# Routed attention and a Hyena gate on one core: q turned by VectorE, its loads and those of k, v, masks and reciprocals cut anew

## The chip, the cores and the metric

One core of a Trainium2 chip. Its engines: TensorE (PE, with its weight loads as PEld), VectorE (DVE), ScalarE (ACT), GpSimd (POOL) and SyncE (SP); sixteen DMA engines move data between HBM and the on-chip memory (SBUF). Matrix products end in PSUM banks, from which DVE and ACT take them. The metric is the device time of one execution in microseconds (us), as the median of several runs; lower is better.

## The reference

The kernel computes attention in which a query sees only keys of its own cluster, and passes the result through a Hyena gate:

```python
q_assign = np.argmax(np.einsum('bhsd,hcd->bhsc', q_n, c_n), axis=-1)   # nearest of 16 centroids
k_assign = np.argmax(np.einsum('bhsd,hcd->bhsc', k_n, c_n), axis=-1)
mask = q_assign[:, :, :, None] == k_assign[:, :, None, :]
scores = np.where(mask, scale * np.matmul(q, k.transpose(0, 1, 3, 2)), -1000000000.0)
scores = scores - np.max(scores, axis=-1, keepdims=True)
attn = np.exp(scores)
attn = attn / (np.sum(attn, axis=-1, keepdims=True) + 1e-09)
attn_out = np.matmul(attn, v)                        # [4, 8, 768, 64] -> x [4, 768, 512]
proj = x @ w_proj                                    # x1, x2, x3, 512 columns each
x2_conv = irfft(rfft(x2, axis=1) * rfft(filter_fft, axis=0), axis=1)
out = (x1 * x2_conv * x3) @ w_out                    # [4, 768, 512] float32
```

Batch 4, heads 8, sequence 768, head width 64, model width 512. Inputs and output are float32.

## The kernel before

**Tiling.** The 32 heads are worked in eight groups `n` of four, each of two pairs `pr` of heads; two groups make a batch `b`. A pair has six tiles `sk` of 128 keys. For a tile, PE makes the scores of 768 queries and two heads (bf16, in three banks `u`), ACT takes exp of them into `p` (float32), PE multiplies with `vraw` into the bank pair `pair`, and DVE adds `p` up in `acc` for the denominators. The first sum of a pair, of tiles 0 and 1 (line 699), can be DVE's or POOL's. After batch `b` follows its Hyena part (function `hyena`): projections, a Fourier transform as matrix products, its inverse, the output product; it runs beside the attention of later groups, the last one alone at the end.

**Loading and turning.** `load_qk` loads q (`j` = 0) and k (`j` = 1) of a pair into one of four buffers `qkraw`, `load_v` loads v into one of three buffers `vraw`; all by SP's queue, apart from a few early ones. A group needs four buffers, so a buffer is free for the next group when the present one has been turned. Scores need the width of the head on the partitions:

- q is turned by PE: six transposes of 128x128 per pair against `ident` (line 589), each three of them put into `qkP`/`qkT` by ACT or DVE (line 591, in helper `copy`, lines 245 and 247). The second half of the queries is turned with `ident` reversed, so it stands backwards.
- k of groups 2 to 7 (`TURN`) is turned by DVE in blocks of 32x32 (line 567). For that, k is loaded in runs of 32 numbers: four transfers per pair, each 32 partitions (line 286).
- v of groups 2 to 7 has its rows in an order that fits k's: four transfers of 32 partitions per pair (line 299).

Then `qkT` is cast to bf16 into `augs` (line 595; ACT, DVE or POOL), the operand of the scores.

**Routing.** Similarities to the centroids (line 609), turned and compared on DVE (lines 614 to 624), give a one-hot code `ohB`; with a product against `tri` it becomes two bf16 arrays in `ohT` (lines 635, 637). Eight transfers per group, 16 partitions each (line 474), put them as extra rows into `augs`, where they act as the mask. Of groups 0 and 1 some steps differ.

**Denominators.** For groups 0, 1 and 7 PE sums `acc` (line 716); for the others POOL's queue folds `acc` with adding transfers (line 736). By way of HBM (`dd`, `dp` or `dn`, line 728 to 742) the sums come to `dn`, 12 numbers in each of 128 partitions; DVE takes the reciprocal, it goes to `dr` in HBM (line 750), and two transfers (line 753) spread it as `rb` over 64 partitions for each head. Line 782 multiplies (`osb` + eps) by `rb` into `xT`, the operand of the Hyena part. `hyena` reads the backward half with a reversed view.

**Order.** There is no run-time scheduling. `build` lists all operations with their dependences; the list `ORDER` gives their sequence, each entry five times the operation's number plus the engine (PE, ACT, DVE, POOL, SP). Every engine works through its own part in that order and waits where a dependence is open, DMA issues on SP included: what stands behind a waiting issue waits as well. An operation of POOL marked `lock` waits for the last one of DVE that is marked so.

The k load and the reciprocals' spread, as they stand before:

```python
T.qkraw[s][64 * x + 32 * y:64 * x + 32 * y + 32]...rearrange("p (c d) -> p c d", d=32),
T.k[...+ x].rearrange("(p c) d -> p c d", c=4 * NT)[:, :, 32 * y:32 * y + 32]
...
T.rb[64 * hp:64 * hp + 64], T.dr[os][hp:hp + 1].to_broadcast([64, S])
```

Of the kernel before, what the change touches and what calls it, by code (L numbers as in the profile page):

```python
# [34 lines left out]
TURN = [(n, pr) for n in range(2, NG) for pr in range(2)]  # L35
FIRST = 2
# [191 lines left out]
def build(T):  # L228
# [22 lines left out]
    def ap(h):  # L251
        return bank(h.ids[0])
# [13 lines left out]
    def dma(e):  # L266
        return (T.nc.scalar if e == "ACT" else T.nc.sync).dma_start
# [995 lines left out]
```

## Time and profile before

| | |
|---|---|
| median of 3 runs | 369.12 us (366.23 to 370.4) |
| profiled execution, device time | 363.86 us |
| its span, first to last instruction | 362.1 us |
| mean granted TensorE clock | 0.997 |
| moved by DMA | 46.19 MB in 109,796 packets, 97,640 of them under 512 bytes |

The profile is of one execution. Its groups of instructions give the line, the engine, the operation, what is written from what, shape and count, then the busy time in us and the mean of one in ns, then the idle time of the engine just before them and what ended it. A matmul's end is modelled, so a busy PE is not PE at its peak. The transfers' rows give the issuing queue, the count, KB of each and the median time from issue to landing in us. A queue's share is the time that its packets took, as a share of sixteen engines' time.

### The profile page before, as it was taken

What the parts mean: (1) busy time and instruction counts of PE and PEld (TensorE: products, weight loads), DVE (VectorE), ACT (ScalarE), POOL (GpSimd) and SP (SyncE); (2) the same over time, 40 slices, a digit from 0 to 9 for tenths busy, and PEclk for the clock granted to TensorE, in tenths of its full rate; (3) what the DMA queues carried; (4) which work ended last, traced back from release to release, by engine and by line L of the source; (5) the groups of instructions that cost most, each with busy time, mean ns of one, the idle gap of its engine ahead of it and who ended that gap; (6) DMA issues with size and microseconds to landing.
All of it is one profiled execution on the core that took longest, in us unless ns stands there. A gap on an engine that the chain in (4) does not pass through costs nothing.

```text
span 362.1 us, 8441 instructions
## 1 busy us (share of the span) xinstructions
PE 349.1 (96%) x3197; PEld 200.6 (55%) x3200; DVE 335.0 (93%) x444; ACT 271.4 (75%) x516; POOL 113.0 (31%) x147
## 2 busy tenths in 40 slices
PE   8999996999999999999999999999999999999994
PEld 4555543444655555665455555576556765576672
DVE  6999996998999999999989999998999999999994
ACT  5998876896997987888998865767885677434452
POOL 5350062020003416220420266443112433025830
PEclk9999999999999999999999999999999999999998
DMA  7939796584668778678867779845446731310124
GB/s 175 221 94 168 156 200 140 113 164 114 137 132 152 117 147 135 126 155 143 151 99 171 134 112 176 201 86 118 86 64 175 144 45 46 103 45 3 61 115 176
DMA packets 109796, 46.19 MB, mean 128 GB/s; under 512 B 97640, under 2 KB 103484, under 8 KB 109756
## 3 DMA queue, kind: packets, MB, share of 16 engines
q1 hardware_dynamic: 104844, 35.59, 43.5%
q0 software_dynamic: 2752, 8.98, 17.3%
q10 hardware_dynamic: 2160, 1.08, 1.0%
q8 instruction: 25, 0.41, 0.5%
q14 instruction: 15, 0.12, 0.1%
HBM read 31.59 MB, written 7.40 MB: 108 GB/s over the span
## 4 chain that ended last, share of the span: by engine, by line
PE 75%; DVE 8%; ACT 7%; DMA 6%; issue 2%; SPq 1%; DVEq 0%; ACTq 0%
PE bank L157 31%; PE pair L690 28%; PE bank L817 6%; PE bank L155 2%; PE bank L589 2%; DMA dd<-den 2%; ACT p L679 2%; PE bank L609 2%; ACT p L676 2%; DMA aug<-ohT 1%; ACT aug L245 1%; DMA qkraw<-in_k_dram 1%; ACT ohT L635 1%; DMA qkraw<-in_q_dram 1%; DVE qkP L567 1%
## 5 line engine op out<-in xcount | busy, mean ns | idle before, releaser
L690 PE MATMUL pair<-p,vraw 128*64 128x385 f32 x768 | 142.1, 488 | 0.3 <-ACT osb L706 0.3
L679 ACT ACTIVATE p<-bank 128x512 f32<-128x512 f32 x192 | 110.1, 610 | 24.4 <-PE bank L157 21.3
L703 DVE TENSOR_TENSOR acc<-p,acc 128x1536 f32<-128x1536 f32 x64 | 112.2, 1753 | 2.9 <-ACT p L679 0.2
L157 PE MATMUL bank<-aug,aug 80*64 80x512 bf16 (+3 forms) x724 | 81.6, 326 | 4.8 <-ACT den L722 2.9
L690 PEld LDWEIGHTS pair<-p,vraw 128*64 128x64 f32 x768 | 55.8, 136 | 44.2 <-issue 35.9
L157 PEld LDWEIGHTS <-aug 80*64 80x64 bf16 (+1 forms) x724 | 44.5, 109 | 44.7 <-issue 31.2
L676 ACT ACTIVATE p<-bank 128x512 f32<-128x512 f32 x96 | 57.6, 610 | 7.2 <-PE bank L157 5.8
L736 POOL DMA_DIRECT2D acc<-acc x30 | 23.9, 815 | 97.5 <-DVE acc L703 64.1
L157 PE MATMUL bank<-xT,wpj 128*64 128x384 bf16 x472 | 44.9, 326 | 0.0
L157 PEld LDWEIGHTS <-wpj 128*64 128x64 bf16 x472 | 28.6, 110 | 13.1 <-issue 3.1
L247 POOL CAST aug<-qkP 64x768 bf16<-64x768 f32 x19 | 15.6, 820 | 52.2 <-DVE acc L703 22.3
L245 ACT CAST aug<-qkP 64x768 bf16<-64x768 f32 x37 | 30.6, 828 | 0.6
L847 DVE TENSOR_TENSOR tm<-bank,hm 128x512 f32<-128x512 f32 x44 | 28.3, 682 | 2.3 <-PE bank L452 1.0
L157 PEld LDWEIGHTS <-y 128*64 128x64 bf16 x456 | 23.1, 110 | 12.1 <-issue 2.9
L245 ACT COPY qkP<-bank 128x384 f32<-128x384 f32 x41 | 18.5, 485 | 8.7 <-PE bank L157 5.4
L157 PE MATMUL bank<-wout,y 128*64 128x512 bf16 (+1 forms) x200 | 23.9, 371 | 0.5 <-DVE y L939 0.5
L817 PE MATMUL bank<-wpj,xT 128*64 128x512 bf16 x192 | 22.4, 379 | 0.0
L939 POOL TENSOR_TENSOR y<-yy,x 128x768 bf16<-128x768 f32 x7 | 12.7, 1821 | 30.9 <-DVE yy L934 27.8
L699 POOL TENSOR_TENSOR acc<-p,p 128x1536 f32<-128x1536 f32 x5 | 17.3, 3465 | 6.7 <-ACT osb L706 4.0
L851 POOL TENSOR_TENSOR y<-tm 128x512 bf16<-128x512 f32 x13 | 16.4, 1272 | 9.2 <-DVE acc L703 3.9
L589 PE MATMUL bank<-ident,qkraw 128*128 128x128 f32 x120 | 18.4, 280 | 0.9 <-DMA qkraw<-in_q_dram 0.7
L699 DVE TENSOR_TENSOR acc<-p,p 128x1536 f32<-128x1536 f32 x11 | 19.1, 1740 | 0.0
(180 smaller groups left out, 437.9 us busy)
## 6 DMA issues: line engine op xcount, KB each, us to landing
qkraw<-in_q_dram SPq DMA_DIRECT2D x30, 192.0 KB, 3.8
rb<-dr SPq DMA_DIRECT2D x30, 192.0 KB, 3.1
qkraw<-in_k_dram SPq DMA_DIRECT2D x51, 96.0 KB, 3.3
vraw<-in_v_dram SPq DMA_DIRECT2D x48, 96.0 KB, 4.2
out_dram<-ob SPq DMA_DIRECT2D x9, 512.0 KB, 2.6
acc<-acc POOLq DMA_DIRECT2D x10, 384.0 KB, 4.6
acc<-acc POOLq DMA_DIRECT2D x10, 192.0 KB, 4.3
vraw<-in_v_dram SPq DMA_DIRECT2D x4, 384.0 KB, 4.6
```

The costliest lines, as they stand in the source:

```text
L157: T.nc.tensor.matmul(out[64 * i:64 * i + 64], lhsT[:, 64 * i:64 * i + 64], rhs, start=start, stop=stop)
L245: T.nc.scalar.copy(out, in_)
L589: T.nc.tensor.transpose(ap(h)[:, ts(t, 128)], raw(s, 3 * ch + t), T.ident[:, ::-1] if ch > j else T.ident)
L676: T.nc.scalar.activation(o, ap(h).rearrange("p (a b) -> p a b", a=2), Act.Exp, scale=0.125)
L679: T.nc.scalar.activation(flat(s)[:, lo:lo + 512], ap(h), Act.Exp, scale=0.125)
L690: T.nc.tensor.matmul(o[64 * hp:64 * hp + 64, ch, :385], T.vraw[vs][:, hp, sk * D:(sk + 1) * D], T.p[slots[sk]][:, hp, 384 * ch:384 * ch + ...
L699: alu(e).tensor_tensor(T.acc[os], T.p[slots[0]][:, :, :S], T.p[slots[1]][:, :, :S], op=Alu.add)
L703: T.nc.vector.tensor_tensor(T.acc[os], T.p[slots[sk]][:, :, :S], T.acc[os], op=Alu.add)
L736: op(("POOL", .8), lambda e, rows=rows: T.nc.gpsimd.dma_start(flat_()[:rows], flat_()[rows:2 * rows], accum_op=Alu.add), te, r=[], w=AK, b ...
L817: T.nc.tensor.matmul(ap(h)[64 * i:64 * i + 64], T.xT[xs][:, kt, c:c + 64], T.wpj[:, kt, DM:2 * DM], start=kt == 0, stop=kt == ND - 1)
L847: op(("DVE", .68), lambda e, i=i, cs=cs, r=r, h=h: T.nc.vector.tensor_tensor(T.tm[r][:, cs], ap(h), hmrow(i, (0, 2, 2, 3)[2 * r + cs]), op ...
L851: op({"POOL": 1.5, "DVE": .68}, lambda e, i=i, r=r: alu(e).tensor_tensor(T.y[:, i, r], T.tm[r][:, 0], T.tm[r][:, 1], op=Alu.add if r else ...
```

## The change

For groups 2 to 7, q is now turned by DVE as k is: 12 more turns on DVE, and no transposes and no evacuations for them. q of these groups is loaded with 8 transfers per pair in runs of 32 numbers, and stands forwards in both halves; so line 782 becomes two operations of half the width, the second of which writes backwards, and `xT` is as before. k takes two transfers per pair, v two, the masks four per group, the reciprocals one per pair. In the new loads of q, k and v and in the spread, the source is divided otherwise than the target: for k, a source of 2 x 768 x 32 goes to 64 partitions x 24 x 32.

`ohT` has no memory of its own any more: it lies in that of `sim`, with its two arrays side by side on 64 partitions, so a hit can write it when `sim` has been read, and `sim` waits for the masks' transfers. `den` has two buffers. Some early operations get the lock, the warm-up of PE names the memory that it uses, and a load of `wout` names one more dependence. `LATE` gives the same pairs as before, and `EXTRA` is empty. `ORDER` is new throughout, with 1,932 operations for 1,987; in it 8 first sums are POOL's (5 before), 11 products of line 939 (7 before), and 14 casts (19 before); ACT casts 48 times (37 before), DVE twice (8 before).

```diff
-        turned = j == 1 and (n, pr) in TURN
+        turned = (n, pr) in (TURNQ, TURN)[j]
+        parts = 1 if j else 4
         for x in range(2) if turned else ():
-            for y in range(2):
-                op(("SP", .6), lambda e, x=x, y=y: dma(e)(
-                    T.qkraw[s][64 * x + 32 * y:64 * x + 32 * y + 32].rearrange("p t h d -> p (t h d)").rearrange("p (c d) -> p c d", d=32),
-                    T.k[n // 2, 4 * (n % 2) + 2 * pr + x].rearrange("(p c) d -> p c d", c=4 * NT)[:, :, 32 * y:32 * y + 32]), due,
-                   w=[("qkraw", s, x, y)], byts=130e3, kind="load", after=after, lat=.8)
+            for g in range(parts):
+                def load(e, x=x, g=g):
+                    m = S // parts
+                    rows = (T.q, T.k)[j][n // 2, 4 * (n % 2) + 2 * pr + x, g * m:g * m + m].rearrange("t (y d) -> y t d", y=2)
+                    raw = T.qkraw[s][64 * x:64 * x + 64].rearrange("p t h d -> p (t h d)")[:, 768 // parts * g:768 // parts * (g + 1)]
+                    dma(e)(raw.rearrange("p (c d) -> p c d", d=32), rows)
...
     def load_v(n, pr, due, after=()):
-        for x in range(4) if (n, pr) in TURN else ():
+        for x in range(2) if (n, pr) in TURN else ():
             op(("SP", .6), lambda e, x=x: T.nc.sync.dma_start(
-                T.vraw[(2 * n + pr) % NV][32 * x:32 * x + 32], T.v[n // 2, 4 * (n % 2) + 2 * pr:4 * (n % 2) + 2 * pr + 2].rearrange(
-                    "h (i p t) d -> p i h (t d)", p=4, t=NT)[x]), due, w=[("vraw", (2 * n + pr) % NV, x)], byts=LOAD / 4, kind="load",
-               after=after, lat=.8)
+                T.vraw[(2 * n + pr) % NV][:, x], T.v[n // 2, 4 * (n % 2) + 2 * pr + x].rearrange("(i p t) d -> p i (t d)", p=4, t=NT)),
+               due, w=[("vraw", (2 * n + pr) % NV, x)], byts=LOAD / 2, kind="load", after=after, lat=.8)
...
+                to = slice(64 - 64 * hp, 80 - 64 * hp)
+                if n:
+                    rows = slice(32 * pr + 16 * hp, 32 * pr + 16 * hp + 16)
+                    out.append(op(("SP", .6), lambda e, a=a, hp=hp, rows=rows, to=to: dma(e)(T.aug[a][hp][to], T.ohT[rows]), due + .3 * hp,
+                                  r=OHT + SIM + [("zero", a, j) for j in range(2)], w=[("augm", a, hp, j) for j in range(2)], byts=50e3,
+                                  lat=2.0 if n < 3 else 1.0))
+                    continue
...
-            if (n, pr) in TURN and j:
+            if (n, pr) in (TURNQ, TURN)[j]:
                 if ch == 0:
-                    op(("DVE", .96), lambda e, s=s, z=z: V().transpose(
-                        T.qkP[z // 2][:, ts(1, S)], T.qkraw[s][:].rearrange("p t h d -> p (t h d)").rearrange("p (q t d) -> p t q d", q=4, d=32)),
-                       due, r=[("qkraw", s, h_, y) for h_ in range(2) for y in range(2)], w=qk(z, 0) + qk(z, 1))
+                    op(("DVE", .96), lambda e, s=s, z=z, j=j: V().transpose(
+                        T.qkP[z // 2][:, ts(j, S)], T.qkraw[s][:].rearrange("p t h d -> p (t h d)").rearrange("p (q t d) -> p t q d", q=4, d=32)),
+                       due, r=[("qkraw", s, x, y) for x in range(2) for y in range(4)], w=qk(z, 0) + qk(z, 1))
...
-            for hp in range(2):
-                op(("SP", .6), lambda e, hp=hp: T.nc.sync.dma_start(
-                    T.rb[64 * hp:64 * hp + 64], T.dr[os][hp:hp + 1].to_broadcast([64, S])), te + 9,
-                   r=[("dr", os)], w=[("rb", hp)], byts=196e3)
+            def spread(e):
+                x = T.dr[os][:]
+                T.nc.sync.dma_start(T.rb, bass.AP(tensor=x.tensor, offset=x.offset, ap=[list(x.ap[0]), [0, 64], list(x.ap[1])]))
+            op(("SP", .6), spread, te + 9, r=[("dr", os)], w=[("rb", 0), ("rb", 1)], byts=393e3)
...
+            def weigh(e, a_=a_):
+                for a in range(a_.start, a_.stop) if plain else [a_]:
+                    o, x, r = xv()[:, a], osv()[:, a], (ap(rk[a_.start])[:, :384] if plain else ap(rk[a_.start])[:, :384].unsqueeze(1)) if last else rbv()[:, a]
+                    if plain:
+                        o, x, r = (y.rearrange("p (t n) -> p t n", n=128) for y in (o, x, r))
+                        o = o[:, :, ::-1] if a else o
+                    T.nc.vector.scalar_tensor_tensor(o, x, eps(), r, op0=Alu.add, op1=Alu.mult)
...
+    T.aug = [[tl([128, 2, S], BF16, f"aug{i}{hp}") for hp in range(2)] for i in range(3)]
+    T.augs = [[[T.aug[i][hp][:, j] for j in range(2)] for hp in range(2)] for i in range(3)]
...
+    words = T.sim[:].rearrange("p a b -> p (a b)").bitcast(BF16)
+    T.ohT, T.ohT0 = words[:64].rearrange("p (j s) -> p j s", j=2), words[:, :S]
```

More of the change, by code (lines that the diff above doesn't have):

```diff
@@ L35 @@
 TURN = [(n, pr) for n in range(2, NG) for pr in range(2)]
+TURNQ = TURN
+LATE = [(n, pr) for n in (0, 1, NG - 1) for pr in range(2)]
+EXTRA = {}
 FIRST = 2
@@ L282, in load_qk @@
         src = lambda: (T.q, T.k)[j][n // 2, 4 * (n % 2) + 2 * pr:4 * (n % 2) + 2 * pr + 2].rearrange("h (p t) d -> p t h d", t=NT)
-        turned = j == 1 and (n, pr) in TURN
+        turned = (n, pr) in (TURNQ, TURN)[j]
+        parts = 1 if j else 4
         for x in range(2) if turned else ():
-            for y in range(2):
-                op(("SP", .6), lambda e, x=x, y=y: dma(e)(
-                    T.qkraw[s][64 * x + 32 * y:64 * x + 32 * y + 32].rearrange("p t h d -> p (t h d)").rearrange("p (c d) -> p c d", d=32),
-                    T.k[n // 2, 4 * (n % 2) + 2 * pr + x].rearrange("(p c) d -> p c d", c=4 * NT)[:, :, 32 * y:32 * y + 32]), due,
-                   w=[("qkraw", s, x, y)], byts=130e3, kind="load", after=after, lat=.8)
+            for g in range(parts):
[4 more added lines that the diff above has]
+                    dma(e)(raw.rearrange("p (c d) -> p c d", d=32), rows)
+                op(("SP", .6), load, due, w=[("qkraw", s, x, g)] if parts > 1 else [("qkraw", s, x, i) for i in range(4)],
+                   byts=260e3 / parts, kind="load", after=after, lat=.8)
         for x in range(2) if not turned else ():
@@ L306, in load_v @@
             T.vraw[(2 * n + pr) % NV], T.v[n // 2, 4 * (n % 2) + 2 * pr:4 * (n % 2) + 2 * pr + 2].rearrange(
-                "h (p t) d -> p h (t d)", t=NT)), due, w=[("vraw", (2 * n + pr) % NV, x) for x in range(4)], byts=LOAD, kind="load",
+                "h (p t) d -> p h (t d)", t=NT)), due, w=[("vraw", (2 * n + pr) % NV, x) for x in range(2)], byts=LOAD, kind="load",
            after=after, lat=.8 if n > 1 else 0.0)
@@ L464, in spectrum @@
                                        T.uv2[:, e, m], start=(m == 0), stop=(m == 2))
+    OHT = [("ohT", j, ch) for j in range(2) for ch in range(2)]
+    SIM = [("sim", ch, pr) for ch in range(2) for pr in range(2)]
     def masks(n, prs, due):
@@ L545, in first_masks @@
         op(("PE", .4), ohT, due + 1.0, r=[("oh", pr), "identb"], w=[h2], alloc=h2)
-        op(("DVE", .68), lambda e: V().tensor_scalar(r64(T.ohT), r64(ap(h2).bitcast(BF16))[:, :S], r64(T.mka), r64(T.mkb),
+        op(("DVE", .68), lambda e: V().tensor_scalar(r64(T.ohT0), r64(ap(h2).bitcast(BF16))[:, :S], r64(T.mka), r64(T.mkb),
                                                      op0=Alu.mult, op1=Alu.add), due + 1.1, r=[h2, "mk"],
-           w=[("ohT", pr)], free=[h2])
+           w=OHT + [("sim", ch, pr) for ch in range(2)], free=[h2])
         return masks(0, [pr], due + 1.2)
@@ L576, in tr2 @@
                         T.nc.tensor.transpose(bank(h.ids[i // 4])[:, ts(i % 4, 128)], raw(ss[i // NT], i % NT), T.ident[:, ::-1] if 3 <= i < NT else T.ident)
-                op(("PE", 1.42), tr2, due, r=[("qkraw", s, x, c) for s in ss for x in range(2) for c in range(2)] + ["ident"], w=[h], alloc=h)
+                op(("PE", 1.42), tr2, due, r=[("qkraw", s, x, c) for s in ss for x in range(2) for c in range(4)] + ["ident"], w=[h], alloc=h)
                 for c in range(3):
@@ L589, in tr @@
                         T.nc.tensor.transpose(ap(h)[:, ts(t, 128)], raw(s, 3 * ch + t), T.ident[:, ::-1] if ch > j else T.ident)
-                op(("PE", .58 if n == 0 else .36), tr, due, r=[("qkraw", s, x, c) for x in range(2) for c in ((0, 1) if n else (ch,))] + ["ident"] + ["cold"] * (n == 0), w=[h], alloc=h)
+                op(("PE", .58 if n == 0 else .36), tr, due, r=[("qkraw", s, x, c) for x in range(2) for c in (range(4) if n else (ch, ch + 2))] + ["ident"] + ["cold", ("wpj", 0)] * (n == 0), w=[h], alloc=h)
                 op(EV384 if n != 1 else {"ACT": .48}, lambda e, z=z, ch=ch, h=h: copy(e, T.qkT[z][:, ch], ap(h)[:, :384]),
@@ L594, in routing, with cast @@
                 for hp in range(2):
-                    op({"ACT": .82, "DVE": .65, "POOL": .95}, lambda e, a=ring(n, pr), hp=hp, j=j, z=z: copy(
-                        e, T.augs[a][hp][j][64 * hp:64 * hp + 64],
-                        T.qkT[z][64 * hp:64 * hp + 64].rearrange("p a b -> p (a b)")), due + 8 if n else due + 6,
+                    def cast(e, a=ring(n, pr), hp=hp, j=j, z=z):
+                        copy(e, T.augs[a][hp][j][64 * hp:64 * hp + 64], T.qkT[z][64 * hp:64 * hp + 64].rearrange("p a b -> p (a b)"))
+                    op({"ACT": .82, "DVE": .65, "POOL": .95}, cast, due + 8 if n else due + 6,
                        r=qk(z, 0) + qk(z, 1) + [("zero", ring(n, pr), j)],
@@ L637, in hits @@
                         V().tensor_scalar(o, x, -1.0 if j else -BIG, 0.0 if j else -BIG, op0=Alu.mult, op1=Alu.max if j else Alu.add)
-                op({"ACT": .47, "DVE": .55}, hits, due - 1.6 + .1 * ch, r=[h], w=[("ohT", j, ch)], free=[h])
+                op({"ACT": .47, "DVE": .55}, hits, due - 1.6 + .1 * ch, r=[h], w=[("ohT", j, ch), ("sim", ch, j)], free=[h])
         masks(n, range(2), due + 1.3)
@@ L651, in attention @@
         last = (n, pr) == (NG - 1, 1)
+        extra = EXTRA.get((n, pr), 0)
         os, o3 = kt % 2, (2 * n + pr) % 3
@@ L693, in pv @@
                                            start=(sk == 0), stop=(sk == NT - 1))
-            op(("PE", 1.3), pv, due, r=[("p", slots[sk], u) for u in range(3)] + [("vraw", vs, x) for x in range(4)] + ["eps"] +
+            op(("PE", 1.3), pv, due, r=[("p", slots[sk], u) for u in range(3)] + [("vraw", vs, x) for x in range(2)] + ["eps"] +
                ([ob] if sk else []), w=[ob], alloc=None if sk else ob, kind="pv")
@@ L855, in hyena @@
             op(("ACT", .83), lambda e: T.nc.scalar.activation(T.neg, T.inv[:].rearrange("p (c b) x -> p c b x", c=2)[:, :, 2:], Act.Copy, scale=-1.0), A(80),
-               r=INV, w=["neg"] + [("qkraw", 0, x, c) for x in range(2) for c in range(2)])
+               r=INV, w=["neg"] + [("qkraw", 0, x, c) for x in range(2) for c in range(4)])
         gs, inv = [], []
@@ L1070, in weights @@
                 T.wout[:, i], T.w_out.rearrange("(t p) m -> p t m", p=128)[:, i]), 118 + 7 * i,
-                w=[("wout", i)] + [("fw", 2, 0), ("fw", 2, 1)] * (i == 0), byts=262e3, after=[first[0]], kind="load")
+                w=[("wout", i)] + [("fw", 2, 0), ("fw", 2, 1)] * (i < 2), byts=262e3, after=[first[0]], kind="load")
     WPJ = [("wpj", i) for i in range(ND)]
@@ L1202 @@
     T.dn, T.rb, T.dp = tl([128, 12], F32, "dn"), tl([128, S], F32, "rb"), tl([128, ROWS, 12], F32, "dp")
-    T.den = tl([128, 384], F32, "den")
+    T.den = [tl([128, 384], F32, f"den{i}") for i in range(2)]
     T.dd = [dram.tile([ROWS, 2 * S], F32, name=f"dd{i}") for i in range(2)]
```

56 lines of the change are left out of this document (28 added, 28 removed), and 162 rows, old and new, of the table ORDER.

## The prediction

> **What bounds the kernel now.** I read the engine totals first, then the chain of waits, then the stages, then the transfers.
>
> ```profile
> span 362.1 us, 8441 instructions
> PE 349.1 (96%) x3197; PEld 200.6 (55%) x3200; DVE 335.0 (93%) x444; ACT 271.4 (75%) x516; POOL 113.0 (31%) x147
> PE 75%; DVE 8%; ACT 7%; DMA 6%; issue 2%; SPq 1%; DVEq 0%; ACTq 0%
> 156.00:196.00 40.00, 39.70 (x377) 22.06 (x375) 37.73 (x45) 37.30 (x70) 7.89 (x9) 1.00 0.79 148
> 196.00:236.00 40.00, 39.95 (x352) 21.88 (x351) 38.47 (x53) 27.95 (x54) 18.15 (x16) 1.00 0.80 153
> q1 hardware_dynamic: 104844, 35.59, 43.5%
> q0 software_dynamic: 2752, 8.98, 17.3%
> ```
>
> The kernel is bound by PE, with DVE close behind (93%); transfers make 6% of the chain. The two stage rows (from:to us, length, busy PE, PEld, DVE, ACT, POOL, granted clock, DMA share, GB/s) say the same of the middle, and one thing more: there the sixteen DMA engines are already busy 79 to 80% of the time, mostly on SP's queue, q1. An edit that takes work from PE pays; one that makes transfers longer has little room. The loads of groups 2 to 7 lie here:
>
> ```profile
> L286 SPq DMA_DIRECT2D qkraw<-in_k_dram x48: 565/640/4904, 34.2 to 240.9; - x48
> qkraw<-in_q_dram SPq DMA_DIRECT2D x30, 192.0 KB, 3.8
> qkraw<-in_k_dram SPq DMA_DIRECT2D x51, 96.0 KB, 3.3
> ```
>
> The first k load of group 2 is issued at 34.2 us, the last of group 7 at 240.9 us. It lands 3.3 us later, so 362.1 - 244.2 = 118 us of work follow.
>
> **The compute that moves.** The rows that price it:
>
> ```profile
> L589 PE MATMUL bank<-ident,qkraw 128*128 128x128 f32 x120 | 18.4, 280 | 0.9 <-DMA qkraw<-in_q_dram 0.7
> L567 DVE STREAM_TRANSPOSE qkP<-qkraw 128x768 f32<-128x768 f32 x12 | 11.4, 960 | 0.0
> L245 ACT COPY qkP<-bank 128x384 f32<-128x384 f32 x41 | 18.5, 485 | 8.7 <-PE bank L157 5.4 <-PE bank L589 3.0
> L782 DVE SCALAR_TENSOR_TENSOR xT<-osb,rb 128x768 bf16<-128x768 f32 x15 | 15.2, 1012 | 0.6 <-DMA rb<-dr 0.6
> L782 DVE SCALAR_TENSOR_TENSOR xT<-osb,bank 128x384 bf16<-128x384 f32 x2 | 1.2, 612 | 0.1
> L245 ACT CAST aug<-qkP 64x768 bf16<-64x768 f32 x37 | 30.6, 828 | 0.6
> L247 DVE CAST aug<-qkP 64x768 bf16<-64x768 f32 x8 | 4.4, 550 | 0.1
> L699 DVE TENSOR_TENSOR acc<-p,p 128x1536 f32<-128x1536 f32 x11 | 19.1, 1740 | 0.0
> L699 POOL TENSOR_TENSOR acc<-p,p 128x1536 f32<-128x1536 f32 x5 | 17.3, 3465 | 6.7 <-ACT osb L706 4.0 <-ACT x L245 2.4 <-DVE y L851 0.2
> L939 DVE TENSOR_TENSOR y<-yy,x 128x768 bf16<-128x768 f32 x5 | 4.8, 953 | 0.2 <-POOL yy L934 0.2
> L939 POOL TENSOR_TENSOR y<-yy,x 128x768 bf16<-128x768 f32 x7 | 12.7, 1821 | 30.9 <-DVE yy L934 27.8
> ```
>
> PE loses the q transposes of six groups, 12 pairs of heads with 6 each: 72 of 120, that is 72/120 x 18.4 = 11.0 us, most of it on the path. ACT and DVE lose their 24 evacuations (24 x 0.485 = 11.6 us). DVE gets 12 more turns, 12 x 0.960 = 11.5 us, and 11 of the weighings of line 782 become two of half width: 11 x (2 x 0.612 - 1.012) = 2.3 us; that the second half is now written backwards is in no row, and I take nothing for it, with 11 x 0.6 = 7 us as the other end, were its time doubled. Read off the new order (a number is five times the operation's place plus its engine), DVE is relieved elsewhere: three first sums go to POOL (-3 x 1.740 = -5.2), four products of line 939 (-4 x 0.953 = -3.8), six casts (-6 x 0.550 = -3.3). That is +1.5 us for DVE, still under PE. POOL takes 3 x 3.465 + 4 x 1.821 = 17.7 us and has 113 of 362 filled; ACT takes casts of 0.828 us for what it loses. The double `den`, the locks on small early operations and the masks' new place in `sim` (a group lies between its writers) I cost at nothing, within 1 us: cover is POOL's idle time and the 36 us of a group. If the transfers cost nothing, this alone gives 363.9 - 11.0 = 353 us for the profiled execution.
>
> **The transfers.** This decides. A load of k was 32 target rows from 32 source rows; now it is 64 target rows, with a source whose outermost dimension is 2 (the halves y). A q load has the same 2, in quarters. The reciprocals' source has an outermost 2 before a repeat of 64; v's has 4. One transfer of the kernel before is of that kind: `dn<-dd` (line 730), 4 x 32 x 12 into 128 rows. Its opposite is `dr<-dn` (line 750), the same 128 packets of 48 bytes, with 128 rows on both sides. First `dr<-dn` in the window 64.27 to 64.50 us, then `dn<-dd` in 58.65 to 59.00 us; each digit is the mean busy share of sixteen engines, in tenths, over a fortieth of the window:
>
> ```profile
> DMA  0002464657778654555776355433430221101000
> DMA packets 144, 0.01 MB, mean 27 GB/s; under 512 B 144, under 2 KB 144, under 8 KB 144
> q1 hardware_dynamic: 144, 0.01, 39.9%
> ...
> DMA  0101121322911221010000000101212122222232
> DMA packets 90, 0.00 MB, mean 12 GB/s; under 512 B 90, under 2 KB 90, under 8 KB 90
> q1 hardware_dynamic: 90, 0.00, 18.2%
> ```
>
> The first is through in 0.23 us, 128 packets and 16 completions, up to 8 tenths of the engines at once. The second has moved fewer than 90 packets after 0.35 us and stands at 2 tenths, under 4/16, but for one slice: it runs on four engines. So the outermost source dimension of 4 confines it, however many target rows there are. By the same reading q, k and the reciprocals go to two engines, v to four. The Trainium skill, "DMA: Bandwidth & Descriptors", section "Why a DMA increments its semaphore by 16 and not by 1", says it as a rule: the number of engines is the largest one up to 16 that divides the slowest dimension of both sides. The trace agrees, 4 and 16. Were it the target alone that counts, the sum would stay at 353 us; that is a rival below.
>
> What a packet costs, from windows in which one kind ran (nearly) alone: a k load, 79.17 to 79.82 us; a reciprocal, 318.5 to 319.5; v, 131.85 to 132.60; and last 30 to 250 us for everything.
>
> ```profile
> DMA packets 823, 0.10 MB, mean 159 GB/s; under 512 B 823, under 2 KB 823, under 8 KB 823
> q1 hardware_dynamic: 823, 0.10, 101.6%
> ...
> q1 hardware_dynamic: 99, 0.26, 69.5%
> ...
> q1 hardware_dynamic: 102, 0.13, 70.6%
> ...
> q1 hardware_dynamic: 80284, 23.17, 50.1%
> q0 software_dynamic: 2400, 7.51, 23.1%
> vraw<-in_v_dram SPq DMA_DIRECT2D x41, 96.0 KB, 3.7
> rb<-dr SPq DMA_DIRECT2D x20, 192.0 KB, 3.4
> ```
>
> - k: 1.016 x 16 x 650 ns / 823 = 12.8 ns per 128-byte packet. A load of 96 KB already kept sixteen engines full.
> - A pair of heads has 2 x 768 x 2 = 3,072 such packets of k. q's rows of 256 bytes are cut into as many. Per group of two pairs 12,288 packets, 6,144 on each of two engines: 6,144 x 12.8 = 79 us. The cheapest packet I have, 48 bytes in `dr<-dn` (0.399 x 16 x 230 / 144 = 10.2 ns), makes 63 us.
> - Reciprocals: 84 packets of 3,072 bytes (99 less 15 completions), 0.695 x 16 x 1,000 / 84 = 132 ns; two transfers per group, 64 packets on each engine: 2 x 64 x 0.132 = 17 us.
> - v: 86 data packets, 0.706 x 16 x 750 / 86 = 98 ns; four transfers per group, 32 packets on each of four engines, these two among them: 4 x 32 x 0.098 = 12.5 us.
> - All else stays spread. Of 73.2% x 220 = 161 us of an engine in 30 to 250 us, k's 36,864 packets take 30, q's 18,432 at about k's price at least 15, twenty reciprocals 11, forty v loads 16; some 85 us are left, 14 per group.
>
> Together 79 + 17 + 12.5 + 14 = 122 us per group, at the low end 63 and about half of the rest, 85. The rest was timed while sixteen engines competed, so I take a value nearer the upper end, 114. A group lasts 206.7/6 = 34 us before (34.2 to 240.9): nothing hides this. SP issues about as many as before (per group 16 for q, 4 for k, 4 for v, 4 masks, 2 reciprocals, against 4, 8, 8, 8 and 4), 0.64 us each, no bound. But its queue is in order: each step of the chain from `dd` to `rb` waits for the one before, behind loads on those two engines, and the loads behind it wait on SP. That stretches a group by up to 20 us.
>
> The sum: the four buffers of `qkraw` hold one group, so the loads of a group wait for the turns of the group before, and DVE, which works in written order, stands at each turn until they land. 34 + 6 x 114 + 118 = 836 us; the 11 us off PE would lie under these waits and save nothing. The range per group, 85 to 142, gives 662 to 1,004. The profiled execution has 363.9 us, 1.8 more than its span, the median of the runs is 369.1: 836 + 1.8 + 5 is 843, and I say 840.
>
> **Rivals.**
> 1. The target's rows count, and sixteen engines carry all: 353 us, 358 against the median. For it speaks that 64 target rows would divide well; against it the second window above. PE's relief is then real, DVE's 1.5 us more is covered. Chance 0.06, all faster.
> 2. Sixteen engines, but q's packets double: 18,432 more x 12.8 / 16 = 15 us on engines that are 80% busy in 156 to 236 us, DVE at 93% waits for turns, and the gain is given back: 366 to 375. Chance 0.03, two thirds within 1%.
> 3. Two engines, but short packets on them go faster than any row shows, as sixteen engines share one memory: at half of 12.8 ns, and the rest at half too, 39 + 22 = 61 us per group, 34 + 6 x 61 + 118 = 518 us. Chance 0.06; against it, 48-byte packets take 10.2 ns and 128-byte packets only 12.8.
> 4. Two engines and a chain that runs hop by hop: SP stops at each of eight hops per group for a drained queue, 8 x 3.3 us more over the 122, 149 us per group, over 1,000 us. Chance 0.05.
>
> **Numbers.** The forecast has 0.80. Range 620 to 1,000: it leaves out the rivals, 0.20. About 1% is what a measurement of this kernel can tell from no change. Faster by over 1%: rival 1, 0.06; within 1%: two thirds of rival 2, 0.02; slower: all else, 0.92.
>
> **What would show it.** Right: the q and k rows of the transfers land in 8 us and more, where 96 KB took 3.3; the DMA row stands at 1 to 3 tenths from 40 us on; the idle time before line 567 on DVE and before the scores on PE is ended by `qkraw` and goes to hundreds of us; L589 has 48. Wrong: q and k landing in 3 to 4 us, a DMA row of 7 to 9 tenths and a span near 351. A right mechanism with a wrong price shows as a share of about 2/16 and a span of 520 or 1,000.

## The result, and the profile after

The changed kernel takes 734.65 us (median of 4 runs, 733.6 to 737.0); the kernel before, on the same chip, 367.68 us. The ratio is 1.998, 95% interval 1.982 to 2.013: the time doubles. The profiled execution has 733.6 us, 1.7 more than its span.

The page of the kernel after, from its head (engine totals, the PEclk and DMA rows in tenths over 40 slices, the queues, and the chain by engine and by line):

```profile
span 731.9 us, 8408 instructions
...
PE 406.3 (56%) x3198; PEld 219.1 (30%) x3198; DVE 334.1 (46%) x448; ACT 276.0 (38%) x506; POOL 132.4 (18%) x152
...
PEclk9977768576857757866669677785875778899999
DMA  8344221111321412313325232332333522432003
...
q1 hardware_dynamic: 121242, 35.36, 22.3%
...
SPq 48%; DMA 24%; PE 16%; DVE 6%; issue 3%; POOL 2%; ACT 0%; POOLq 0%; DVEq 0%
SPq L292 33%; PE bank L158 7%; DMA rb<-dr 6%; PE pair L704 4%; SPq L304 4%; SPq L482 4%; DMA dd<-acc 4%; DMA dr<-dn 3%; DMA dn<-dd 3%; PE bank L840 3%; DMA qkraw<-in_q_dram 3%; SPq L771 3%; DMA dp<-dd 2%; DMA qkraw<-in_k_dram 2%; SPq L757 2%
```

DVE and ACT do about the work of before (334 and 276 us against 335 and 271), POOL the 19 us more that the change gave it; only the span is twice as long. The bytes on SP's queue are the same within 1% (35.36 MB, 35.59 before), and so, nearly, is the time that its packets took: 22.3% of 731.9 us is 163 us of sixteen engines, 43.5% of 362.1 was 158. From the second slice on the DMA row is mostly 1 to 4 where it was 6 to 9. The chain, 75% PE before, is now 48% SPq and 24% DMA, and a third of the whole span is the issue of the new q and k loads, line 292. Engines with nothing to do, DMA engines mostly idle, and a chain made of loads: this fits transfers that use a few of the sixteen; the experiments below test it.

Where each engine stands, from the groups of instructions (busy us, mean ns, then idle time before them and what ended it):

```profile
L580 DVE STREAM_TRANSPOSE qkP<-qkraw 128x768 f32<-128x768 f32 x24 | 23.0, 966 | 106.3 <-DMA qkraw<-in_k_dram 49.7
L158 PE MATMUL bank<-aug 128*64 128x512 bf16 (+3 forms) x768 | 104.9, 379 | 190.7 <-DMA aug<-sim 112.1
L806 DVE SCALAR_TENSOR_TENSOR xT<-osb,rb 128x384 bf16<-128x384 f32 (+1 forms) x26 | 16.6, 673 | 76.9 <-DMA rb<-dr 76.9
```

Line 580 is the turn, 806 the weighing. DVE's turn stood 0.0 us before and now 106.3; the weighing 0.6 and now 76.9. PE's scores wait 190.7 us, most of it not for a load but for the masks (`aug<-sim`), small transfers that were issued behind loads.

The issues of the new loads in the trace of the kernel after (engine, operation, count, then the ns of one issue as least/median/most, and the first and last start in us):

```profile
L292 SPq DMA_DIRECT2D qkraw<-in_q_dram x96: 502/1761/14674, 22.6 to 590.9; - x96
L292 SPq DMA_DIRECT2D qkraw<-in_k_dram x24: 512/1734/8944, 23.3 to 575.0; - x24
```

From the first load of group 2 to the last of group 7 it takes 590.9 - 22.6 = 568.3 us, 94.7 per group, where it took 34. And one issue on SP, 0.64 us before, takes 1.76 in the median and up to 14.7. The chain of waits of the kernel after, in the window 234 to 334 us (start, us, what), shows what this does:

```profile
243.72 10.66 SPq L292
254.42 2.23 SPq L292
256.69 1.82 SPq L292
258.51 0.04 issue
258.55 1.76 SPq L292
260.36 7.18 SPq L292
267.58 1.74 SPq L292
269.32 0.06 issue
269.43 1.77 SPq L482
```

SP spends 25 us in the issues of six loads (the one at 258.55 us is of k, the others are of q), with no wait between them; only then does it reach the masks of line 482. What that is to PE stands in its timeline, in the window 255 to 320 us (start, us, what, and in brackets the idle time before and its end):

```profile
272.94 1.92 PE L158 MATMUL bank<-aug 80*64 80x512 bf16 x10 [23.84 <-DMA aug<-sim]
```

### The profile page after: what moved, and what is told of

It reads as the page before. It is cut to its first block, busy times and chain, and to the rows that moved or that the text cites. A ratio compares the mean times of both kernels' runs of the same rounds, so it can differ in the third digit from the quotient of the medians.

```text
span 731.9 us, 8408 instructions
## 1 busy us (share of the span) xinstructions
PE 406.3 (56%) x3198; PEld 219.1 (30%) x3198; DVE 334.1 (46%) x448; ACT 276.0 (38%) x506; POOL 132.4 (18%) x152
## 3 DMA queue, kind: packets, MB, share of 16 engines
q1 hardware_dynamic: 121242, 35.36, 22.3%
## 4 chain that ended last, share of the span: by engine, by line
SPq 48%; DMA 24%; PE 16%; DVE 6%; issue 3%; POOL 2%; ACT 0%; POOLq 0%; DVEq 0%
SPq L292 33%; PE bank L158 7%; DMA rb<-dr 6%; PE pair L704 4%; SPq L304 4%; SPq L482 4%; DMA dd<-acc 4%; DMA dr<-dn 3%; DMA dn<-dd 3%; PE bank L840 3%; DMA qkraw<-in_q_dram 3%; SPq L771 3%; DMA dp<-dd 2%; DMA qkraw<-in_k_dram 2%; SPq L757 2%
## 5 line engine op out<-in xcount | busy, mean ns | idle before, releaser
L158 PE MATMUL bank<-aug 128*64 128x512 bf16 (+3 forms) x768 | 104.9, 379 | 190.7 <-DMA aug<-sim 112.1
L704 PE MATMUL pair<-p,vraw 128*64 128x385 f32 x768 | 169.6, 564 | 19.7 <-DMA vraw<-in_v_dram 14.5
L158 PEld LDWEIGHTS <-aug 128*64 128x64 bf16 (+1 forms) x768 | 52.6, 125 | 248.7 <-issue 139.6
L704 PEld LDWEIGHTS pair<-p,vraw 128*64 128x64 f32 x768 | 68.1, 160 | 76.7 <-issue 61.9
L580 DVE STREAM_TRANSPOSE qkP<-qkraw 128x768 f32<-128x768 f32 x24 | 23.0, 966 | 106.3 <-DMA qkraw<-in_k_dram 49.7
L158 PE MATMUL bank<-xT,wpj 128*64 128x384 bf16 x504 | 55.3, 344 | 3.0 <-DVE x L920 2.8
L806 DVE SCALAR_TENSOR_TENSOR xT<-osb,rb 128x384 bf16<-128x384 f32 (+1 forms) x26 | 16.6, 673 | 76.9 <-DMA rb<-dr 76.9
L713 POOL TENSOR_TENSOR acc<-p,p 128x1536 f32<-128x1536 f32 x8 | 27.7, 3457 | 88.9 <-DMA dd<-acc 32.6
L158 PE MATMUL bank<-inv,y 128*64 128x192 bf16 x272 | 15.5, 252 | 22.0 <-POOL y L874 22.0
L622 PE MATMUL bank<-qkP,cbd 128*32 128x384 f32 x112 | 15.7, 694 | 21.7 <-DVE hm L436 14.4
```

The lines of the kernel that those rows point to most:

```text
L158: T.nc.tensor.matmul(out[64 * i:64 * i + 64], lhsT[:, 64 * i:64 * i + 64], rhs, start=start, stop=stop)
L704: T.nc.tensor.matmul(o[64 * hp:64 * hp + 64, ch, :385], T.vraw[vs][:, hp, sk * D:(sk + 1) * D], T.p[slots[sk]][:, hp, 384 * ch:384 * ch + ...
L713: alu(e).tensor_tensor(T.acc[os], T.p[slots[0]][:, :, :S], T.p[slots[1]][:, :, :S], op=Alu.add)
```

## The experiments

The theory on record: a load whose source has an outermost dimension of 2 or 4 runs on that many engines. Against it stands that the loss lies in the new order, in the memory that `ohT` and `sim` now share, or in the number of issues. The experiments recut some transfers, and leave order, buffers and arithmetic alone; only the last two do more, one moves issues to POOL, the other splits the weighing. Recut means:

```diff
 # k (and likewise, where it says so, q), in load_qk
-                    dma(e)(raw.rearrange("p (c d) -> p c d", d=32), rows)
+                        for y in range(2):
+                            dma(e)(T.qkraw[s][64 * x + 32 * y:64 * x + 32 * y + 32].rearrange("p t h d -> p (t h d)").rearrange("p (c d) -> p c d", d=32),
+                                   T.k[n // 2, 4 * (n % 2) + 2 * pr + x].rearrange("(p c) d -> p c d", c=4 * NT)[:, :, 32 * y:32 * y + 32])
 # v, in load_v: twice as many, as before the change
-                T.vraw[(2 * n + pr) % NV][:, x], T.v[n // 2, 4 * (n % 2) + 2 * pr + x].rearrange("(i p t) d -> p i (t d)", p=4, t=NT)),
+                T.vraw[(2 * n + pr) % NV][32 * y:32 * y + 32], T.v[n // 2, 4 * (n % 2) + 2 * pr:4 * (n % 2) + 2 * pr + 2].rearrange(
+                    "h (i p t) d -> p i h (t d)", p=4, t=NT)[y]) for y in (2 * x, 2 * x + 1)],
 # the reciprocals, in spread
-                T.nc.sync.dma_start(T.rb, bass.AP(tensor=x.tensor, offset=x.offset, ap=[list(x.ap[0]), [0, 64], list(x.ap[1])]))
+                for hp in range(2):
+                    T.nc.sync.dma_start(T.rb[64 * hp:64 * hp + 64], T.dr[os][hp:hp + 1].to_broadcast([64, S]))
```

The same numbers move in the same runs of 128, 1,536 or 3,072 bytes; only how they are grouped into transfers differs.

**All of them recut.** q like k, so four transfers per pair; the kernel then leaves out the order of q's rows: its queries stand in k's order, and the output is not the reference's. The amount of work is the same.

> The changed kernel with every load of k, q, v and the reciprocals on sixteen engines, at the same number of issues per pair as the kernel before (4 q, 4 k, 4 v, 2 reciprocals). For that, q's rows of groups 2 to 7 are taken in k's order, four transfers of 32 x 24 x 32 per pair, so the queries are permuted and the output is not the reference's; the packets (3,072 of 128 bytes per pair) and all compute are those of the changed kernel. Two-engine theory: nothing but the engines' number was wrong, so the time falls from 735 to that of my first rival, 358 us, at most 375 if q's doubled packets cost what the engines lack. Order theory (the new order, its turns of q on DVE and its waits on SP hold it up): over 550 us.

Measured: 353.03 us (4 runs, 352.84 to 353.28), ratio to the kernel before 0.964 (0.958 to 0.971). Its page and the issues of its q loads:

```profile
span 351.6 us, 8448 instructions
...
PE 340.2 (97%) x3198; PEld 195.7 (56%) x3198; DVE 329.0 (94%) x448; ACT 273.3 (78%) x506; POOL 132.0 (38%) x152
...
DMA  7969989446896989968958978795768341310134
...
q1 hardware_dynamic: 123660, 35.36, 48.6%
```

```profile
L299 SPq DMA_DIRECT2D qkraw<-in_q_dram x48: 560/644/2032, 22.3 to 231.1; - x48
```

The whole loss is gone: 734.65 - 353.03 = 382 us hang on how the sources are cut. The new order, the memory that `ohT` and `sim` share, the turns and the weighings are all still in this kernel. So is every byte; the DMA row stands at 7 to 9 again, and an issue at 0.644 us. PE is 97% busy, with 349.1 - 340.2 = 8.9 us less to do.

**One kind at a time.** Only k recut; only q (like k); only v and the reciprocals.

> The changed kernel with k alone back on sixteen engines (four transfers of 32 rows per pair), q and the rest unchanged. The trace of the changed kernel has a group every 94.7 us. Two-engine theory: 3,072 of 6,144 packets per engine and group go, at 9.4 to 12.8 ns 29 to 39 us, and come back as 2 us on every engine: 6 groups x 27 to 37 = 160 to 220 us less, 515 to 575 us. Order theory: no change over 5%, 700 to 770.

> Only q is cut for sixteen engines (four transfers per pair, 48 in place of 96, its queries left in k's order, so the output is in another order); k, v and the reciprocals stay as changed. If packets on two engines set the price, q is worth what k was worth (q and k have 36,864 packets each): 567 to 597 us, where the run with k alone on sixteen gave 582. If what counted were the number of issues on SP, it would be well under that, 530 or less, as this edit takes 48 issues away where that one added 24.

> The changed kernel with v (four transfers of 32 rows per pair) and the reciprocals (two of 64 rows) back on sixteen engines, q and k on two. Two-engine theory, terms of the prediction at the changed trace's lower pace: 17 and 12.5 us per group, perhaps half as much, on engines that are not always busy, so 6 x 12 to 25 = 70 to 150 us less: 585 to 665 us. If q and k alone set the pace, 700 to 735.

Measured (one execution each): 581.95, 574.76 and 614.67 us. The q loads' issues with k recut, with v and the reciprocals recut, and those of q and k with q recut:

```profile
L297 SPq DMA_DIRECT2D qkraw<-in_q_dram x96: 502/1742/12343, 22.2 to 439.5; - x96
```

```profile
L292 SPq DMA_DIRECT2D qkraw<-in_q_dram x96: 502/1760/10440, 22.7 to 499.3; - x96
```

```profile
L294 SPq DMA_DIRECT2D qkraw<-in_q_dram x48: 559/644/16149, 22.1 to 422.6; - x48
...
L297 SPq DMA_DIRECT2D qkraw<-in_k_dram x24: 518/590/8987, 22.8 to 423.2; - x24
```

The group shrinks from 94.7 us to (439.5 - 22.2)/6 = 69.6 with k recut, to (423.2 - 22.1)/6 = 66.9 with q, and to 79.4 with v and the reciprocals. So k costs 25 us of a group, q 28, v and the reciprocals 15 (each from a single execution; runs of one kernel differ by a few us in all). k and q cost about the same, as they have equally many packets, though q's recutting takes 48 issues away and k's adds 24: packets, not issues, set this price. The three sum to 68, and all together saved 94.7 - (231.1 - 22.3)/6 = 59.9: with all recut a group takes 34.8 us and PE is 97% busy, so PE sets the pace, and the last of the three savings does not show in full.

**How many engines, counted.** The prediction read 128 packets and 16 completions off one transfer: each engine that takes part ends with one packet of its own. So the number of packets on SP's queue tells how many engines a load used. If the merged q, k and spread used 2 each and v 4, recutting k must add 48 x 16 - 24 x 2 = 720 packets, q 48 x 16 - 96 x 2 = 576, v and the spread 48 x 16 - 24 x 4 + 30 x 16 - 15 x 2 = 1,122. The queue's rows, after the change and then with k, with q, and with v and the reciprocals recut:

```profile
q1 hardware_dynamic: 121242, 35.36, 22.3%
```

```profile
q1 hardware_dynamic: 121962, 35.36, 28.1%
```

```profile
q1 hardware_dynamic: 121818, 35.36, 29.0%
```

```profile
q1 hardware_dynamic: 122364, 35.36, 27.2%
```

The differences are 720, 576 and 1,122, to the packet, and for all together 123,660 - 121,242 = 2,418, their sum. The runs with a single merge, below, part the last one: merging the spreads alone takes 450 packets off, in the new order (123,210 for 123,660) and in the old one (104,394 for 104,844), so v has the other 672; merging k alone in the old kernel takes off 720 (104,124). That is the number of engines, shown. It follows the source's outermost dimension, 2 or 4, with 64 or 128 rows in the target. The transfer from which the prediction took its four engines says the same: in the trace before, 132 packets under 512 bytes pass between 58.65 and 59.17 us, the 128 of `dn<-dd` and 4 more.

**One merge put into the kernel before.** If the cut alone does it, it must do it there too, where the order is the old one.

```diff
 # in load_qk of the kernel before: k only
-                    T.qkraw[s][64 * x + 32 * y:64 * x + 32 * y + 32]...,
-                    T.k[...+ x].rearrange("(p c) d -> p c d", c=4 * NT)[:, :, 32 * y:32 * y + 32]), due,
+                    T.qkraw[s][64 * x:64 * x + 64]...,
+                    T.k[...+ x].rearrange("t (y d) -> y t d", y=2)), due,
 # in another kernel: the reciprocals only
-                    T.rb[64 * hp:64 * hp + 64], T.dr[os][hp:hp + 1].to_broadcast([64, S])), te + 9,
+                    T.rb, bass.AP(tensor=T.dr[os][:].tensor, offset=T.dr[os][:].offset, ap=[list(T.dr[os][:].ap[0]), [0, 64], list(T.dr[os][:].ap[1])])), te + 9,
```

> The kernel before with one edit: the two k transfers of a head (halves y) made one, source 2 x 768 x 32, target 64 rows; the second of the two operations issues nothing. Two-engine theory: 3,072 packets per engine and group at 9.4 to 12.8 ns are 29 to 39 us beside 12 to 14 us of other traffic on the same two engines, where a group lasts 34 us: 7 to 19 us too much per group, 366 + 6 x 7 to 19 = 410 to 480 us. Order theory: the old order is kept, so within 2% of before, and a little SP time saved.

> The kernel before with one edit: the reciprocals' two transfers made one, source 2 x 64 x 768, target 128 rows; the second operation issues nothing. Two-engine theory: 64 packets of 3,072 bytes on each of two engines, 7 to 8.5 us instead of 3.1 from issue to landing; line 782 has slack in most pairs, so 0 to 5 us per pair for 15 pairs is too much and I expect 367 to 385 us. If a short transfer on two engines is hidden, within 1%.

Measured: 499.46 us with k merged (2 runs), ratio 1.364 (1.351 to 1.378); 440.37 with the reciprocals merged (4 runs), ratio 1.209 (1.202 to 1.217). Both are dearer than expected, the second by far: 15 issues fewer cost 76 us. The chain of the first, and of the second its chain by line and the weighing among the groups of its instructions:

```profile
PE 36%; SPq 30%; DMA 14%; DVE 11%; issue 4%; ACT 3%; POOL 0%; DVEq 0%; ACTq 0%
```

```profile
DMA rb<-dr 18%; PE bank L157 18%; PE pair L690 16%; PE bank L817 5%; DMA aug<-ohT 4%; DMA dd<-den 2%; ACT p L679 2%; SPq L474 2%; DMA qkraw<-in_k_dram 2%; DVE xT L782 1%; PE bank L589 1%; ACT p L676 1%; DVE acc L703 1%; DMA dp<-dd 1%; PE bank L155 1%
...
L782 DVE SCALAR_TENSOR_TENSOR xT<-osb,rb 128x768 bf16<-128x768 f32 x15 | 15.2, 1015 | 57.4 <-DMA rb<-dr 57.4
```

A k load on two engines holds SP, and with it the masks and denominators behind it. For the reciprocals the rows name another place: DVE, which works in written order, stands at line 782 until they land, 57.4 us in all where it was 0.6, and the chain has `rb<-dr` for 18% of 437.9 us, 79 us, where in the kernel before it is not among the fifteen first. That is about the whole loss. On two engines a spread has 64 packets on each, at the prediction's 132 ns 8.4 us. In the trace DVE waits at ten of the fifteen, and these are weighed 10.0 to 13.4 us after their issue, where a spread landed 3.1 us after it before (median); at the other five something else came last. So it is not 5 us fifteen times: they land some 7 us and more later, and the work between hides a part.

The same merge alone in the new order, with k, q and v recut (q in k's order, so the order of q's rows is again left out):

> The changed order with k, q and v on sixteen engines (the queries left in k's order, so the output is in another order) and only the reciprocals' spread merged, on two engines. If DVE stands at the weighing for each spread, as it did in the old order (76 us for 15 spreads), this gives 410 to 435 us; if the new order leaves them time to land, 353 to 370.

Measured: 424.3 us (one execution), 71 more than with all recut, 4.8 per spread on average. In its groups of instructions:

```profile
L817 DVE SCALAR_TENSOR_TENSOR xT<-osb,rb 128x384 bf16<-128x384 f32 (+1 forms) x26 | 16.6, 673 | 47.2 <-DMA rb<-dr 47.1
```

DVE waits nearly as long as in the old order (57.4 us), and 3.5 with all recut: the new order hides a late spread little better than the old one.

**A version that computes the reference and keeps the gain.** With 32 rows of the target in each transfer, q in its right order needs 16 transfers per pair:

```diff
+                        for y in range(2):
+                            dma(e)(raw[32 * y:32 * y + 32].rearrange("p (c d) -> p c d", d=32),
+                                   T.q[n // 2, 4 * (n % 2) + 2 * pr + x, g * m:g * m + m].rearrange("(p c) d -> p c d", c=NT)[:, :, 32 * y:32 * y + 32])
```

> The changed kernel with k, v and the reciprocals on sixteen engines as in the run before, and q in its right order: each of its eight parts per pair is two transfers of 32 x 6 x 32, so 16 per pair instead of 8, all on SP. Output as the reference. Two-engine theory: engines are free, the time falls from 735 to below 400; what is open is SP's queue, 28 loads, masks and reciprocals and 3 others per pair at 0.6 us, 19 us of the 17 to 18 us that a pair lasts: 360 to 385 us if that binds, 353 to 356 if not. Order theory: over 550 us; the last run has spoken against it.

Measured: 411.18 us, ratio 1.130 (1.121 to 1.138), slower than expected. The chain by engine and by line:

```profile
PE 51%; SPq 21%; DMA 9%; DVE 8%; issue 6%; ACT 2%; POOL 2%; POOLq 0%; DVEq 0%; ACTq 0%
PE bank L158 24%; PE pair L715 17%; SPq L299 13%; SPq L294 4%; DMA qkraw<-in_q_dram 3%; DMA aug<-sim 3%; PE bank L851 3%; DVE acc L728 2%; SPq L314 2%; PE bank L1110 2%; PE bank L633 2%; SPq L493 1%; ACT p L704 1%; DMA dn<-dd 1%; DMA dd<-acc 1%
```

Here the sixteen engines are free, and the number of issues on SP looks like the price: 192 for q in place of 48, 0.60 us each in the median, are 87 us more of SP's time, and the kernel takes 411.18 - 353.03 = 58 us longer. To test it, half of them are issued by POOL:

```diff
-                            dma(e)(raw[32 * y:32 * y + 32]...
+                            (T.nc.gpsimd if y else T.nc.sync).dma_start(raw[32 * y:32 * y + 32]...
```

> As the run before, but the second half (y = 1) of each q part is issued on POOL's queue: SP has 8 issues fewer per pair, POOL 96 more in all, at some 0.8 us each 77 us on an engine that is busy 132 us. If SP's queue binds in the run before, this is faster than it, 353 to 360 us; if POOL's waits for free buffers hold up its sums and products, slower than it, 365 to 400.

Measured: 361.42 us (4 runs, 358.23 to 365.54), ratio 0.989 (0.977 to 1.0005). Fifty of the 58 us are back, so the issues on SP were the price; whether this is faster than the kernel before, the runs can't tell. POOL pays 58.5 us for it, beside other work (among the groups of instructions):

```profile
L299 POOL DMA_DIRECT2D qkraw<-in_q_dram x96 | 58.5, 671 | 15.7 <-DVE qkP L591 14.8
```

Last, q in k's order by four transfers per pair, put right afterwards: every step up to the weighing treats queries alike, so the weighing can write each to its place, in six operations of 128 columns with a stride.

```diff
-                        o, x, r = (y.rearrange("p (t n) -> p t n", n=128) for y in (o, x, r))
-                        o = o[:, :, ::-1] if a else o
+                        for t in range(3):
+                            o1 = o[:, ts(t, 128)].rearrange("p (i q) -> p q i", q=4)
+                            x1, r1 = (y[:, ts(t, 128)].rearrange("p (q i) -> p q i", q=4) for y in (x, r))
+                            T.nc.vector.scalar_tensor_tensor(o1[:, ::-1, ::-1] if a else o1, x1, eps(), r1, op0=Alu.add, op1=Alu.mult)
+                        continue
```

> All loads of k, q, v and the spread are cut so that no source begins with a 2 or a 4; q is loaded like k, four transfers per pair, so its queries stand in k's order, and line 806 puts them back: six operations of 128 columns per pair, written with a stride, in place of two of 384. The two-engine theory with SP's issues as the second bound: 353 us (the run with the queries left in k's order) plus at most what DVE gets more, 11 pairs x (6 x 0.35 - 2 x 0.6) = 10 us if all of it showed, so 353 to 363 us, faster than the kernel before. If the strided write were slow (1 us per operation), DVE would pass PE and the run would come to 375 us and more.

Measured: 361.16 us (6 runs, 360.81 to 362.5), ratio 0.987 (0.983 to 0.991): 1.3% faster than the kernel before, a small gain, but one whose interval leaves out 1. Its weighing among the groups of instructions:

```profile
L818 DVE SCALAR_TENSOR_TENSOR xT<-osb,rb 128x128 bf16<-128x128 f32 x66 | 21.1, 491 | 0.0
```

It costs 361.16 - 353.03 = 8 us of the 13 by which that kernel was faster than the one before (366.24 on the same chip). The rows agree: one operation of 128 columns takes 0.49 us alone, but they overlap, and the six of a pair keep DVE busy for 21.1/11 = 1.92 us, where two of 384 columns took 12.5/11 = 1.14 with all recut; eleven times the difference is 8.6 us.

## Why the prediction was right, and which terms were off

**The mechanism held.** The likeliest case said two engines for q, k and the reciprocals, four for v, read off `dn<-dd` and `dr<-dn`. The packet counts show 2, 2, 2 and 4. The row of `dn<-dd` was weak ground: it has three slices over 4/16 (two of 3 tenths, one of 9), not one as the prediction says; the counts are better ground. The Trainium skill, "DMA: Bandwidth & Descriptors", section "Why a DMA increments its semaphore by 16 and not by 1", has the rule (the largest number up to 16 that divides the slowest dimension of both sides); every one of the counts here agrees with it.

**The compute held.** Rival 1's 353 us was the sum of the compute part alone, and the kernel with all sources recut takes 353.03, though with the queries out of order; in order it was 361. Two terms inside it were off: PE lost 8.9 us for 11.0, and DVE lost 335.0 - 329.0 = 6.0, where +1.5 was worked out. The operations that the prediction listed come to +0.3 in that kernel's trace, and writing backwards costs nothing (0.607 us for a half, 0.612 before); the rest, 6.3, are small operations that also left DVE and that it did not list, three operations `y<-tm` of 2.0 us among them. The span fell by 362.1 - 351.6 = 10.5 nevertheless, since PE also idled less, 11.4 us for 13.0.

**The sum.** It said 34 + 6 x 114 + 118 = 836 us; the trace has 22.6 + 6 x 94.7 + 141.0 = 731.9. The groups are 116 us too long over six, the start 11 too long, the end 23 too short. The time lies 13% under the 840 forecast, and that it came so near is in part luck: 114 was a choice between 85 and 122, the error at the end goes the other way, and SP's long issues, which the sum left out, cost little on top, as far as the waiting in an issue is the same draining of packets that the sum had counted.

- *q and k, 79 us per group.* This term was mis-sized. A window of the kernel after in which nearly only these loads ran, 310 to 320 us:

```profile
DMA  1111151111111111111111111111111111111111
DMA packets 2128, 0.29 MB, mean 29 GB/s; under 512 B 2127, under 2 KB 2127, under 8 KB 2127
...
q1 hardware_dynamic: 2127, 0.27, 17.3%
```

  The engines stand at 1 tenth, which fits 2/16 = 0.125, and two of them put 2,127 packets through in 10 us: 9.4 ns for a packet on one engine. The share still says 0.173 x 16 x 10,000 / 2,127 = 13.0 ns, what I took. The error was to read a queue's share as time for which an engine is taken: it adds up the times of packets, and they overlap on one engine. The row that I quoted for the k load had the warning in it, a share of 101.6%. At 9.4 ns, 6,144 packets make 58 us per group; the experiments give 25 + 28 = 53. Counted the same way, the old kernel's window of 79.17 to 79.82 us gives 650 x 16 / 823 = 12.6 ns, but its engines were partly idle in the first half. From 79.50 to 79.82 us, where the DMA row stands at 8 and 9 tenths but for one slice, 483 packets passed: 320 x 16 / 483 = 10.6 ns, which would have made 65 us. So most of the error could have been seen in the trace before. The rest, 9.4 ns on two engines for 10.6 on sixteen, is what was right of rival 3's reason; its halved price was not. What the sixteen share, no run here shows.
- *v and the reciprocals, 29.5 us.* Recutting both saves 15 in the group. The price of a long packet, 132 ns, fits: 64 of them are 8.4 us, and the quickest of the spreads that DVE waited for was there 10.0 us after its issue. But I put it wholly into the engines' queue, and missed that DVE pays for a late spread by itself: 71 to 76 us even where the loads are quick.
- *"SP issues about as many as before, 0.64 us each, no bound".* Wrong for this state. An issue takes 1.76 us, and a q load puts 192 packets on each of two engines: 192 x 9.4 ns = 1.8 us. With sixteen engines an issue of twice as many packets took 0.644. So it is not the writing of the packets that is slow; the numbers fit an issue that must wait until what stands ahead has drained. A k load, with 768 packets on each of two engines, shows it: its own issue at 258.55 us takes 1.76 us, but the one behind it 7.18, and 768 x 9.4 ns is 7.2 us. What is issued behind it does not matter: at 519.57 us a `dr<-dn`, 0.31 us at its quickest, takes 7.60 behind a k load. That SP waits for room in the queue is my reading of them; no run shows what it waits for. "Its queue is in order" was right, and this is how it works: 48% of the chain is SP's queue.
- *The end, 118 us.* From the last issue it was 362.1 - 240.9 = 121.2 before and is 141.0. Of the 19.8, 8.4 lie between that issue and the last turn (15.4 us, 7.0 before) and 11.4 behind it, where masks and reciprocals are late as well: DVE waits 15.9 us for `rb<-dr` there.
- *The allowance of 5 us* between profiled execution and median was 1 (734.65 for 733.6).

**The signs.** Seen: a DMA row of mostly 1 to 3 tenths; 48 transposes on PE left, now at line 602; waits before the turn of over a hundred microseconds (106.3, of which `qkraw` ends 91). Seen otherwise: before the scores it is the masks, queued behind loads, that come last, not `qkraw`. The landing times of the loads are not in the page, so "8 us and more" stays open.

**The rivals.** Rival 2's double packets for q showed nothing: with sixteen engines DVE's turns do not wait, and the DMA row at 7 to 9 bears them. Rival 4's hop by hop, eight times 3.3 us on top, did not come: 94.7 us per group is under the 122 of the plain sum, and still under it with q and k at 9.4 ns, 58 + 17 + 12.5 + 14 = 101.5.

## What to carry to other kernels

Before merging transfers, read the outermost dimension of both sides: a merge that halves the issues but puts a 2 in front leaves two of sixteen engines; 15 spreads merged in this way cost 76 us here. Check how many engines ran by counting packets on the queue: each engine that takes part adds one completion. And price packets by how many pass in a window in which the engines are busy throughout, not by the queue's share, which adds up packets that overlap.

## What the hardware showed beside it

PE's busy time grew by 57 us although 72 transposes left it: 406.3 for 349.1. Stretches of 10 us of the kernel after (from:to, length, busy PE, PEld, DVE, ACT, POOL with counts, granted clock, DMA share, GB/s):

```profile
254.00:264.00 10.00, 0.00 (x0) 0.00 (x0) 0.00 (x0) 0.00 (x0) 0.00 (x0) 0.50 0.25 35
264.00:274.00 10.00, 1.06 (x8) 0.63 (x10) 0.00 (x0) 0.00 (x0) 0.00 (x0) 0.50 0.20 34
274.00:284.00 10.00, 10.00 (x78) 5.00 (x76) 6.22 (x9) 7.00 (x14) 4.03 (x3) 0.85 0.25 39
...
294.00:304.00 10.00, 9.96 (x82) 5.17 (x82) 3.43 (x4) 8.36 (x14) 0.81 (x1) 0.99 0.38 73
```

While PE waits for masks, the granted clock is 0.50; the 8 matmuls that end the wait still run at it; 10 us of full work bring it back to 0.85 on average, and later to 0.99. The mean over the kernel is 0.769, against 0.997 before. The Trainium skill, "TensorE: Matmul & The Clock Gate", section "Part 1: The HAM clock gate (the "warmup" mystery)", states a half-rate clock after an idle window and the full one after a busy window, each of about 3.4 us; the trace agrees with the two levels. So a wait for a transfer is paid a second time in slower matmuls: a scores matmul took 379 ns on average, and 326 in the last experiment, whose clock was 0.995.
